# A spectral mixer with an MLP on one core: the first batch's transform as one product, and work moved to GpSimd

## The chip, the cores and the metric

The kernel runs on one core of one Trainium2 chip. The metric is device time in microseconds: the median of three runs is 2610.31 us (2610.21 to 2612.57). The engines are TensorE (PE; PEld is its weight load), VectorE (DVE), ScalarE (ACT), GpSimd (POOL) and SyncE (SP), which here only issues DMAs.

## The reference

For each of 8 batches `x` (3072 positions by 256 channels) goes through a Fourier transform along the positions, a complex 256x256 channel mix with a bias and a soft threshold, and the inverse transform. Then every position goes through an MLP, 256 to 2048 with softplus, back to 256.

```python
X = np.fft.rfft(x, axis=1)
Yr = Xr @ w_r - Xi @ w_i + b_r
Yi = Xr @ w_i + Xi @ w_r + b_i
Yr = np.sign(Yr) * np.maximum(np.abs(Yr) - 0.01, 0.0)   # Yi likewise
y = np.fft.irfft(Y, n=x.shape[1], axis=1)
h = y @ w_in
g = np.maximum(h, 0.0) + np.log1p(np.exp(-np.abs(h)))
out = g @ w_out
```

## The kernel before

**Stages.** The transform of 3072 = 96 x 32 positions is done in two stages. `s1` transforms along 96; its result is kept in SBUF as `a0` for batch 0 and goes through DRAM (`a_dr`) for the others. `s3` (after `load_a` has gathered one pair of groups, `gp` = 0 to 11, out of `a0` or `a_dr`) transforms along 32 with the constants `g1`; `mix` multiplies with the channel weights, adds the bias (for batch 0 `bias0`) and shrinks; `s4` and `s5` are the way back. `s5` leaves tokens, each split into a rounded high and a low fp32r part.

**MLP.** It runs in keys (batch, block pair, one eighth of the hidden width), four steps a key: `slot_products` issues the first product and softplus, `slot_second` the second product. Each product is three matmuls, high x high, high x low, low x high (`mm3`, L249 to L252). First products are Strassen-like: seven combinations of weights and tokens. After batch 0's start the MLP's products fill PE, and the transform of later batches is strewn between.

**Weights.** `w_in` and `w_out` arrive as 64-bit words and are turned into fp32 high and low parts by `split_w`, a generator that goes on one `yield` per step: L196 to L203 take the words apart into two summands `t` and `u`, L219 to L223 add them (with the Strassen combinations of w_in in L228 to L231), L233 rounds the high part, L235 takes the low part, and the result is stored to DRAM, from where later keys stream it. The table `turns` gives for each weight the step at which its conversion begins and at which it is loaded. While `early` holds (steps before -1), the adds of L219 to L223 run on POOL and the product of L203 on DVE; from then on the adds run on DVE and L203 on POOL.

**First transform.** Batch 0 and the columns from 10 on of batch 1, and all later batches, use `s1_four`: x is loaded as two halves of 48 rows, partitions 0 to 47 and 64 to 111 (`load_first`, `load_four`; a memset clears partitions 32 to 63), `fold` makes their sum and difference on DVE (L324, L325, 112x512), and eight matmuls with 48 rows follow (L339). For batch 0, `load_first` finds each of eight loads a place in a buffer that is free at the start. The first eight to ten columns of batch 1 use `s1`, one 96-row product with the constants `f_sb` (L281). ACT copies the results (L348 into `a0`, L283, L352).

**What sets the order.** Everything is written out step by step: `product` puts a transform's matmuls at a step, `at` puts loads, folds and other calls at a step, and the loop at the end of the kernel issues, in each step, the MLP's products, the conversions, the transform product, then what `at` put there. Each engine and each DMA queue works in that order. Steps before 0 are the first batch's transform; `t0` is the first step. SP's queue carries nearly all DMAs; POOL's queue carries half of the `a0` loads from gp 3 on and half of `s4`'s results.

Lines that matter below: L197 (first DVE instruction of a conversion), L478 and L475 (first `z` of a mix: bias added, gp 0 and later), L119 (low part of a split), L378 (`s3`), L362 (`load_a`), L596 and L612 (low parts of tokens), L694 (`add`, one input in PSUM), L710 (`low`, both inputs in SBUF).

Of the kernel before, what the change touches and what calls it, by code (L numbers as in the profile page):

```python
# [10 lines left out]
F32 = mybir.dt.float32  # L11
# [6 lines left out]
P = 128  # L18
# [16 lines left out]
def tile_spectral_mixer_mlp(ctx, tc, x, w_r, w_i, bias, bias_0, w_in, w_out, f, f_hi, f_lo, g1, g3, g3_hi, g3_lo, hm, out):  # L35
# [34 lines left out]
    y1 = sb.tile([P, 14 * BLK], F32, tag="y1", name="y1", bufs=1)  # L70
    a1 = y1[:N1, :4 * 512].rearrange("p (i n) -> p i n", i=4)
    g1_0 = y1[:, 4 * 512:10 * 512].rearrange("p (g n) -> p g n", g=NG)
# [109 lines left out]
    def split_w(which, m2, own):  # L182
# [29 lines left out]
        ahead = bool(early)  # L212
        e = g if ahead else v
        if which:

            tm, um = [a.rearrange("p (k m n) -> p m k n", k=2, m=2) for a in (t, u)]
            a21 = tm[:, 1, 0]
            o = [src[:, i * P:(i + 1) * P] for i in range(7)]
            e.tensor_tensor(out=src[:, A11 * P:(A11 + 2) * P].rearrange("p (k n) -> p k n", k=2), in0=tm[:, 0], in1=um[:, 0], op=ALU.add)  # L219
            e.tensor_tensor(out=a21, in0=a21, in1=um[:, 1, 0], op=ALU.add)  # L220
            e.tensor_tensor(out=o[A22], in0=tm[:, 1, 1], in1=um[:, 1, 1], op=ALU.add)
        else:
            e.tensor_tensor(out=src, in0=t, in1=u, op=ALU.add)  # L223
        if ahead:
            yield
            yield
# [40 lines left out]
    def load_x(b, c):  # L267

        xt = sb.tile([P, 512], F32R, tag=("gh", "gl")[c % 2], name="xt", bufs=3).bitcast(F32)[:N1]
        nc.sync.dma_start(  # L270
            xt.rearrange("p (n c) -> p n c", n=2),
            x[b].rearrange("(p n) c -> p n c", n=N2)[:, 2 * c:2 * c + 2, :],
        )
        xs[b, c] = xt

    def s1(b, c):

        if c == 0:
            a_dr[b] = dram.tile([N1, N2, D], F32, tag="a", name="a_dr")
        ps = psf()  # L280
        nc.tensor.matmul(ps, f_sb, xs.pop((b, c)), start=True, stop=True)  # L281
        a = a1[:, c % 4] if c < 8 else g1_0[:N1, 4 * (c - 8) + 16:4 * (c - 8) + 20].rearrange("p g n -> p (g n)")
        nc.scalar.copy(a, ps[:N1, :])  # L283
        store(a_dr[b][:, 2 * c:2 * c + 2, :], a.rearrange("p (n c) -> p n c", n=2), ("a", b))

# [10 lines left out]

    def load_first(c):

        place = ('w64', 'raw', 'w64', 'l', 'x1', 'w1', 'w1', 'dpt')[c]
        if place == "x1":  # L300
            xt = fours[1]
        elif place == "dpt":
            xt = dpt
        elif place == "raw":
            xt = sb.tile([P, 1024], F32, tag="raw", name="x4", bufs=1)
        elif place == "w64":
            xt = sb.tile([P, 1024], F32, tag="w64", name="x4")
        elif place == "l":
            xt = sb.tile([P, 2 * 768], F32R, tag="l", name="x4", bufs=1).bitcast(F32)
        else:  # L310
            xt = sb.tile([P, 2 * 7 * P], F32R, tag="w1", name="x4").bitcast(F32)
        s = sb.tile([P, 512], F32, tag=("a", "d")[c % 2], name="plus")
        rows = x[0].rearrange("(h p n) c -> p h n c", h=2, n=N2)
        nc.vector.memset(xt[32:64, :1024], 0.0)
        for i in (1, 0):
            n = 4 * c + 2 * i
            nc.sync.dma_start(xt[64 * i:64 * i + 48, :1024].rearrange("p (h n c) -> p h n c", h=2, n=2), rows[:, :, n:n + 2, :])
        xs[0, c, "four"] = xt[:, :512], xt[:, 512:1024], s

    def fold(b, c):  # L320

        lo, hi, both = [t[:112] for t in xs[b, c, "four"]]
        e = nc.vector
        e.tensor_tensor(out=both, in0=lo, in1=hi, op=ALU.add)  # L324
        e.tensor_tensor(out=hi, in0=lo, in1=hi, op=ALU.subtract)  # L325
        stored["x", b, c] += 1

    def s1_four(b, c):
# [4 lines left out]
        _, minus, plus = xs.pop((b, c, "four"))  # L333
        if b:
            stored["four", c % 2] += 1
        banks = psf(), psf()
# [8 lines left out]
        for i, ps in enumerate(banks):  # L345
            n = 4 * c + 2 * i
            if b == 0:
                nc.scalar.copy(a0[:, n:n + 2, :].rearrange("p n c -> p (n c)"), ps)  # L348
                stored["a", b] += 1
                continue  # L350
# [433 lines left out]
    with tc.manual_schedule():  # L784
        nc.scalar.preload_act_table_set("softplus")


        fill, steps, before = {}, {}, {}
        nc.sync.dma_start(f2, f_hi)
        nc.gpsimd.dma_start(g3_sb, g3)  # L790
# [39 lines left out]

        first = [("s1", 0, c) for c in range(8)] + [("s1", 1, c) for c in range(4)]
        for i in range(NP + 3):
# [10 lines left out]
        for t, (what, b, i) in enumerate(first, t0):  # L843
            if what == "s1" and b == 0:
                product(t, s1_four, b, i)
                at(t0 - 1, load_first, i)
            elif what == "s1":
# [24 lines left out]
        last = first.index(("s4", 0, NP - 1)) + t0
        begun = first.index(("s4", 0, 7)) + t0
# [56 lines left out]
def _constants():  # L930
# [95 lines left out]
```

## Time and profile before

| | |
|---|---|
| median of 3 runs | 2610.31 us (2610.21 to 2612.57) |
| profiled execution | span 2607.2 us (the page gives no other time of it) |
| PE busy | 2566.7 us, 98% |
| DVE busy | 1687.6 us, 65% |
| ACT busy | 1669.9 us, 64% |
| POOL busy | 167.0 us, 6% |
| mean granted clock of TensorE | 0.998 |

The profile is of one execution. Times are us from the span's start. "Idle before <-X" is the time that an engine stood before an instruction, and what ended it. A busy PE is not PE at its peak. PEclk is the share of full speed that was granted to TensorE.

### The profile page before, as it was taken

How to read it: one execution, taken by the hardware profiler on the slowest of the kernel's cores; microseconds unless marked ns; L12 is line 12 of the kernel's file. 1: busy time of each engine (PE TensorE's matmuls, PEld its weight loads, DVE VectorE, ACT ScalarE, POOL GpSimd, SP SyncE). 2: the span in 40 equal slices, each digit the busy share in tenths (PEclk: the TensorE clock that was granted, in tenths of full speed). 3: DMA queues.
4: the chain of work that ended last, by engine and by line, in shares of the span. 5: the costliest groups of instructions: out<-in, count | busy, mean ns of one | idle time of the engine just before them, and what ended most of it. 6: DMA issues, size and time to landing. Idle time of an engine off the chain costs nothing.

```text
span 2607.2 us, 36350 instructions
## 1 busy us (share of the span) xinstructions
PE 2566.7 (98%) x13193; PEld 2125.6 (82%) x13193; DVE 1687.6 (65%) x2836; ACT 1669.9 (64%) x3025; POOL 167.0 (6%) x198
## 2 busy tenths in 40 slices
PE   7899999999999999999999999999999999999999
PEld 5677878888788888888888888888888888888887
DVE  6888775676566765667656667466774666645454
ACT  4576666666666666666666666666666666666665
POOL 2320000000000000000000000000000000000000
PEclk9999999999999999999999999999999999999999
DMA  8975555755546556475555665556645545445543
GB/s 214 273 238 193 173 187 164 220 174 176 186 162 199 181 173 190 162 205 179 170 191 174 186 195 163 180 176 187 207 155 173 182 155 190 140 159 183 174 150 113
DMA packets 187087, 472.56 MB, mean 181 GB/s; under 512 B 22252, under 2 KB 88844, under 8 KB 186908
## 3 DMA queue, kind: packets, MB, share of 16 engines
q1 hardware_dynamic: 183084, 466.79, 56.9%
q0 software_dynamic: 2912, 2.58, 0.4%
q8 instruction: 105, 1.72, 0.3%
q10 hardware_dynamic: 912, 0.85, 0.1%
q14 instruction: 74, 0.61, 0.1%
HBM read 383.09 MB, written 82.71 MB: 179 GB/s over the span
## 4 chain that ended last, share of the span: by engine, by line
PE 93%; DVE 3%; DMA 2%; ACT 1%; issue 1%; SPq 0%; ACTq 0%; POOL 0%; DVEq 0%
PE pso L250 14%; PE pso L252 13%; PE pso L251 13%; PE psc L250 7%; PE psc L252 7%; PE psc L251 7%; PE pse L250 5%; PE pse L252 5%; PE pse L251 5%; PE psf L573 5%; PE psf L252 3%; PE psf L251 3%; PE psf L250 3%; PE psf L378 3%; PE psf L339 2%
## 5 line engine op out<-in xcount | busy, mean ns | idle before, releaser
L710 DVE TENSOR_TENSOR gl<-t,gh 128x512 fp32r<-128x512 f32 x768 | 532.2, 693 | 328.9 <-ACT gh L704 326.5
L689 ACT COPY t<-psc 128x512 f32<-128x512 f32 x576 | 337.2, 585 | 524.3 <-PE psc L252 521.8
L694 DVE TENSOR_TENSOR t<-pse,t 128x512 f32<-128x512 f32 x576 | 396.1, 688 | 402.3 <-ACT t L689 276.4
L250 PE MATMUL pso<-gh,w 128*128 128x512 f32 x1536 | 620.6, 404 | 0.0
L252 PE MATMUL pso<-gh,w 128*128 128x512 f32 x1536 | 599.5, 390 | 0.0
L251 PE MATMUL pso<-gl,w 128*128 128x512 f32 x1536 | 599.2, 390 | 0.0
L704 ACT CAST gh<-t 128x512 fp32r<-128x512 f32 x768 | 476.8, 621 | 60.8 <-PE pso L252 37.4
L700 ACT ACTIVATE t<-t 128x512 f32<-128x512 f32 x576 | 365.1, 634 | 69.2 <-DVE t L694 68.0
L250 PEld LDWEIGHTS pso<-gh,w 128*128 128x128 f32 x1536 | 289.3, 188 | 90.6 <-issue 41.4
L252 PEld LDWEIGHTS pso<-gh,w 128*128 128x128 f32 x1536 | 288.3, 188 | 62.5
L251 PEld LDWEIGHTS pso<-gl,w 128*128 128x128 f32 x1536 | 289.4, 188 | 49.2
L250 PE MATMUL psc<-y_sb,w 128*128 128x512 f32 x768 | 300.9, 392 | 5.4 <-ACT t L689 5.1
L252 PE MATMUL psc<-y_sb,w 128*128 128x512 f32 x768 | 299.9, 391 | 0.0
L251 PE MATMUL psc<-y_sb,w 128*128 128x512 f32 x768 | 299.1, 389 | 0.0
L612 POOL TENSOR_TENSOR y_sb<-raw,y_sb 128x512 fp32r<-128x512 f32 x69 | 104.9, 1520 | 2147.4 <-ACT y_sb L609 2147.4
L250 PE MATMUL pse<-y_sb,w 128*128 128x512 f32 x576 | 226.2, 393 | 4.4 <-DVE t L694 4.4
L251 PE MATMUL pse<-y_sb,w 128*128 128x512 f32 x576 | 224.5, 390 | 0.6 <-DVE y_sb L596 0.6
L252 PE MATMUL pse<-y_sb,w 128*128 128x512 f32 x576 | 224.4, 390 | 0.0
L250 PEld LDWEIGHTS psc<-y_sb,w 128*128 128x128 f32 x768 | 144.2, 188 | 38.7 <-ACT t L689 7.9
L252 PEld LDWEIGHTS psc<-y_sb,w 128*128 128x128 f32 x768 | 144.3, 188 | 31.2
L251 PEld LDWEIGHTS psc<-y_sb,w 128*128 128x128 f32 x768 | 144.4, 188 | 30.0
L511 DVE TENSOR_TENSOR shrunk<-z,cl 64x256 f32<-64x256 f32 x336 | 141.1, 420 | 6.2
(168 smaller groups left out, 3365.1 us busy)
## 6 DMA issues: line engine op xcount, KB each, us to landing
w<-w_dr SPq DMA_DIRECT2D x190, 896.0 KB, 7.6
w<-w_dr SPq DMA_DIRECT2D x185, 512.0 KB, 3.5
out_y<-ot SPq DMA_DIRECT2D x96, 256.0 KB, 2.8
x<-in_x SPq DMA_DIRECT2D x116, 192.0 KB, 7.3
dp<-d_dr SPq DMA_DIRECT2D x57, 384.0 KB
ap<-a_dr SPq DMA_DIRECT2D x168, 128.0 KB, 6.0
d_dr<-d SPq DMA_DIRECT2D x84, 256.0 KB, 2.1
a_dr<-a SPq DMA_DIRECT2D x102, 192.0 KB, 3.0
```

The source lines that it names most:

```text
L250: nc.tensor.matmul(ps, wh, xh, start=start, stop=False, skip_group_check=more)
L251: nc.tensor.matmul(ps, wh, xl, start=False, stop=False, skip_group_check=more)
L252: nc.tensor.matmul(ps, wl, xh, start=False, stop=stop, skip_group_check=more)
L378: nc.tensor.matmul(xv[:, g, k], t[:, g, k * P:(k + 1) * P], g1_t[:, g].rearrange("p (c s) -> p c s", c=2), start=True, stop=True,)
L511: v.tensor_tensor(out=t[dst], in0=z[src], in1=cl[src], op=ALU.subtract)
L573: nc.tensor.matmul(ps[:, t - blk * BLK:t - blk * BLK + n], d_sb[b, blk // 2, n2 // 4][0][:, n2 % 4, k * P:(k + 1) * P], d_sb[b, blk // 2, ...
L612: eng.tensor_tensor(out=lo, in0=raw[j], in1=hi.bitcast(F32), op=ALU.subtract)
L689: nc.scalar.copy(t, banks[bank])
L694: nc.vector.tensor_tensor(out=t, in0=banks[bank], in1=t, op=ALU.add)
L700: nc.scalar.activation(t, banks[bank] if bank else t, AF.Softplus)
L704: nc.scalar.copy(gh, ct[key, what])
L710: nc.vector.tensor_tensor(out=gl, in0=ct.pop((key, what)), in1=gh.bitcast(F32), op=ALU.subtract)
```

## The change

- Batch 0's first transform uses `s1`, 16 products of 96 rows with `f_sb`, in place of eight times `s1_four`. `load_first`, its memsets and its folds are gone. The 16 loads of x go to 96 partitions each, at places of their own: `xt` buffers, the `dp` buffer, and `x1`; four of them are issued by ACT. `f` is padded by 16 columns, so that the results lie in partitions 16 to 111 as before.
- `t0` is 8 steps earlier (16 products in place of 8). The loads of `g1`, `bias0`, the mix's weights and `f2` stand at other steps; ACT's table load stands behind its DMA issues.
- `fold` runs on POOL for batches 1 and 2.
- The adds of `split_w` run on POOL also for conversions inside the MLP, and what follows the adds comes one step later there.

```diff
-    a1 = y1[:N1, :4 * 512].rearrange("p (i n) -> p i n", i=4)
+    a1 = y1[:16 + N1, :4 * 512].rearrange("p (i n) -> p i n", i=4)
...
         ahead = bool(early)
-        e = g if ahead else v
+        e = g
...
             e.tensor_tensor(out=src, in0=t, in1=u, op=ALU.add)
+        yield
         if ahead:
-            yield
             yield
         if which:
             v.tensor_tensor(out=o[S1], in0=a21, in1=o[A22], op=ALU.add)
...
     def load_x(b, c):
-        xt = sb.tile([P, 512], F32R, tag=("gh", "gl")[c % 2], name="xt", bufs=3).bitcast(F32)[:N1]
-        nc.sync.dma_start(
+        if b or c < 6:
+            xt = sb.tile([P, 512], F32R, tag=("gh", "gl")[c % 2], name="xt", bufs=3).bitcast(F32)
+        elif c < 14:
+            xt = dps[:, (c - 6) * 512:(c - 5) * 512]
+        else:
+            xt = fours[1][:, (c - 14) * 512:(c - 13) * 512]
+        xt = xt[:N1]
+        (nc.sync if b or c % 2 == 0 or c > 8 else nc.scalar).dma_start(
             xt.rearrange("p (n c) -> p n c", n=2),
...
         nc.tensor.matmul(ps, f_sb, xs.pop((b, c)), start=True, stop=True)
+        if b == 0:
+            nc.scalar.copy(a0[:, 2 * c:2 * c + 2, :].rearrange("p n c -> p (n c)"), ps)
+            stored["a", b] += 1
+            return
...
-    def load_first(c):
...
     def fold(b, c):
         lo, hi, both = [t[:112] for t in xs[b, c, "four"]]
-        e = nc.vector
+        e = nc.gpsimd if b < 3 else nc.vector
...
-        nc.scalar.preload_act_table_set("softplus")
-        nc.sync.dma_start(f2, f_hi)
+        nc.sync.dma_start(f_sb, f)
...
-        first = [("s1", 0, c) for c in range(8)] + [("s1", 1, c) for c in range(4)]
+        first = [("s1", 0, c) for c in range(16)] + [("s1", 1, c) for c in range(4)]
...
-                at(max(t0 - 1, t - (5 if i < 4 else 16)), load_x, b, i)
+                at(t - 16 if b and i >= 4 else t0 + 4 + i if b else t0 - 1, load_x, b, i)
...
-                at(max(t - 7, t0 + 8), load_a, b, i)
+                at(max(t - 7, t0 + 16), load_a, b, i)
...
-        for c in range(8):
-            at(max(t0 - 1, t0 + c - 1), fold, 0, c)
-        for t, i, j in ((t0 + 7, 0, 4), (t0 + 8, 4, 12), (t0 + 14, 12, NG)):
+        for t, i, j in ((t0 + 7, 0, 4), (t0 + 18, 4, 12), (t0 + 20, 12, NG)):
             at(t, nc.sync.dma_start, g1_0[:, i:j], g1[:, NG + i:NG + j])
-        at(t0 + 5, nc.sync.dma_start, bias0, bias_0)
+        at(t0 + 19, nc.sync.dma_start, bias0, bias_0)
         at(12, nc.sync.dma_start, bias_sb, bias)
         for k in range(2):
-            at(t0 + 6 + k, load_mix, k)
-            at(t0 + 10 + k, split_mix, k)
-        at(t0 + 2, nc.sync.dma_start, f_sb, f)
+            at(t0 + 10 + k, load_mix, k)
+            at(t0 + 17 + k, split_mix, k)
+        at(-30, nc.sync.dma_start, f2, f_hi)
...
+        at(t0 - 1, nc.scalar.preload_act_table_set, "softplus")
...
-    f = np.pad(f, ((0, 0), (0, P - N1)))
+    f = np.pad(f, ((0, 0), (16, P - N1 - 16)))
```

SP's queue between batch 0's x and the first conversion, before. `x_96` holds `f_sb` and `bias0`, `y_79` holds `g1_0` and the results of batch 1's `s1`, `ap` receives the `a0` loads (source `a_78`), `dpt` a weight.

```order
L914 DMA x_96<-in_f 96x128
L270 DMA xt<-in_x 96x512 x3
L914 DMA x_96<-in_bias 128x512
L270 DMA xt<-in_x 96x512
L145 DMA stage<-in_w_r 128x2x256
L914 DMA y_79<-in_g 128x512
L145 DMA stage<-in_w_i 128x2x256
L362 DMA ap<-a_78 128x1x256 x6
L914 DMA y_79<-in_g 128x1024
L179 DMA dpt<-in_w_in 128x2x512
```

The same queue in the changed kernel.

```order
L889 DMA y_79<-in_g 128x512
L145 DMA stage<-in_w_r 128x2x256
L145 DMA stage<-in_w_i 128x2x256
L344 DMA ap<-a_78 128x1x256 x6
L179 DMA dpt<-in_w_in 128x2x512
L104 DMA a_dr<-y_79 96x512
L344 DMA ap<-a_78 128x1x256
L889 DMA y_79<-in_g 128x1024
L104 DMA a_dr<-y_79 96x512
L889 DMA x_96<-in_bias 128x512
L104 DMA a_dr<-y_79 96x512
L889 DMA y_79<-in_g 128x1536
```

The bias load moved from ahead of the six `a0` loads to behind them, and the second part of `g1` from ahead of the first `w_in` load to behind it.

DVE at the start of batch 0's mixes, before: the last fold, the splits of the mix's weights, the low part of the first s3, the first `z`, `cl` and difference, the next low part, and the first conversion.

```order
L325 TENSOR_TENSOR dpt<-dpt 112x512
L119 TENSOR_TENSOR wml<-stage,wmh 128x2x256 x2
L119 TENSOR_TENSOR w_277<-psf,w_277 128x4x128
L478 TENSOR_TENSOR z<-psf,x_96 128x512
L479 TENSOR_SCALAR cl<-z 128x512
L480 TENSOR_TENSOR z<-z,cl 128x512
L119 TENSOR_TENSOR w_287<-psf,w_287 128x4x128
L197 TENSOR_SCALAR wt<-dpt 128x512
```

DVE in the changed kernel, from its first instruction.

```order
L119 TENSOR_TENSOR wml<-stage,wmh 128x2x256 x2
L119 TENSOR_TENSOR w_229<-psf,w_229 128x4x128
L460 TENSOR_TENSOR z<-psf,x_96 128x512
L461 TENSOR_SCALAR cl<-z 128x512
L462 TENSOR_TENSOR z<-z,cl 128x512
L119 TENSOR_TENSOR w_239<-psf,w_239 128x4x128
L197 TENSOR_SCALAR wt<-dpt 128x512
```

The memsets and folds in front are gone; from the splits on, the sequence is the same.

POOL from the last conversion that begins before the MLP, before. `x_96` and `x_97` are the two buffers of `s1_four`'s x.

```order
L219 TENSOR_TENSOR y_79<-wt,wu 128x256
L220 TENSOR_TENSOR wt<-wt,wu 128x128
L221 TENSOR_TENSOR y_79<-wt,wu 128x128
L914 MEMSET x_96 32x1024
L203 TENSOR_TENSOR wu<-y_79,wu 128x512 x4
L158 TENSOR_TENSOR stage<-stage 128x512
```

POOL at the same place in the changed kernel.

```order
L311 TENSOR_TENSOR x_97<-x_97 112x512
L312 TENSOR_TENSOR x_97<-x_97 112x512
L889 MEMSET x_96 32x1024
L203 TENSOR_TENSOR wu<-y_79,wu 128x512
L219 TENSOR_TENSOR y_79<-wt,wu 128x256
L220 TENSOR_TENSOR wt<-wt,wu 128x128
L221 TENSOR_TENSOR y_79<-wt,wu 128x128
L311 TENSOR_TENSOR x_96<-x_96 112x512
L312 TENSOR_TENSOR x_96<-x_96 112x512
L311 TENSOR_TENSOR x_97<-x_97 112x512
L312 TENSOR_TENSOR x_97<-x_97 112x512
L203 TENSOR_TENSOR wu<-y_79,wu 128x512
```

Between the products of L203 stand the folds (L311, L312) and the adds that DVE had.

## Rows read from the trace of the kernel before

**Rows 1.** Windows by stage: each engine's busy us (instructions), PEclk, DMA share, GB/s.
```profile
0.00:109.00 109.00, 86.83 (x542) 65.91 (x542) 82.36 (x139) 51.55 (x102) 33.80 (x60) 0.98 0.84 229
109.00:125.00 16.00, 9.99 (x33) 5.83 (x31) 15.38 (x26) 11.49 (x21) 3.77 (x4) 0.89 1.01 346
125.00:260.00 135.00, 128.90 (x651) 100.80 (x652) 114.30 (x202) 95.80 (x175) 20.06 (x21) 1.00 0.68 218
260.00:2607.20 2347.20, 2340.97 (x11971) 1953.06 (x11970) 1475.60 (x2471) 1511.09 (x2730) 109.38 (x114) 1.00 0.56 176
```

**Rows 2.** The chain that ended last, start: begin, us, what (DMAs to landing).
```profile
12.03 8.25 DMA dpt<-in_x
...
31.32 8.77 DMA dpt<-in_w_in
```

**Rows 3.** Windows of the start: PE, PEld, DVE, ACT, POOL busy, PEclk, DMA share, GB/s.
```profile
4.00:20.00 16.00, 9.78 (x54) 4.21 (x56) 13.89 (x20) 5.79 (x12) 0.00 (x0) 1.00 1.08 195
20.00:26.00 6.00, 5.51 (x22) 1.85 (x16) 1.38 (x2) 3.95 (x8) 0.00 (x0) 1.00 0.93 281
26.00:30.00 4.00, 1.93 (x10) 1.04 (x8) 1.39 (x2) 2.42 (x6) 0.01 (x1) 1.00 0.27 96
```

**Rows 4.** Timeline of the first 32 us: begin, us, instruction, count, [idle before <-releaser].
```profile
10.22 1.12 PE L339 MATMUL psf<-plus,f 48*64 48x512 f32 x2 [10.22 <-DVE plus L324]
...
15.39 1.06 PE L339 MATMUL psf<-plus,f 48*64 48x512 f32 x2
...
17.21 0.59 PE L339 MATMUL psf<-plus,f 48*64 48x512 f32 x2
...
22.84 3.70 PE L281 MATMUL psf<-xt,x 96*128 96x512 f32 x8
...
24.04 5.78 SPq L362 DMA_DIRECT2D ap<-a  x6
```

**Rows 5.** Timeline from 34 to 46 us, the first two mixes.
```profile
36.99 0.69 DVE L478 TENSOR_TENSOR z<-psf,x 128x512 f32<-128x512 f32 x1 [6.00 <-PE psf L252]
...
38.69 1.13 PE L378 MATMUL psf<-y,ap 128*128 128x128 f32 x8 [1.74 <-issue]
...
38.87 0.68 DVE L119 TENSOR_TENSOR w<-psf,w 128x512 fp32r<-128x512 f32 x1
...
40.11 0.43 DVE L197 TENSOR_SCALAR wt<-dpt 128x512 uint32<-128x512 uint32 x1 [0.55 <-DMA dpt<-in_w_in]
...
43.24 0.68 DVE L475 TENSOR_TENSOR z<-psf,x 128x512 f32<-128x512 f32 x1
...
45.98 0.39 PE L252 MATMUL psf<-wmh,w 128*128 128x256 f32 x1 [1.10 <-DVE w L119]
```

**Rows 6.** Timeline of DVE at 86 us.
```profile
86.22 0.43 DVE L197 TENSOR_SCALAR wt<-w 128x512 uint32<-128x512 uint32 x1 [2.18 <-DMA w<-in_w_out]
```

**Rows 7.** DMA issues from 1.0 to 1.7 us: KB each, us to landing.
```profile
x<-in_x SPq DMA_DIRECT2D x1, 192.0 KB, 3.4
```

**Rows 8.** Windows from 30 to 42 us, columns as in rows 3.
```profile
30.00:34.00 4.00, 3.60 (x14) 3.13 (x14) 0.69 (x1) 1.44 (x4) 1.82 (x3) 0.57 0.60 187
34.00:42.00 8.00, 5.99 (x46) 5.61 (x47) 4.16 (x7) 2.25 (x5) 1.29 (x6) 1.00 0.96 277
```

**Rows 9.** Timeline of DVE at 108 us.
```profile
108.44 0.89 DVE L324 TENSOR_TENSOR x<-x 112x512 f32<-112x512 f32 x1
```

**Rows 10.** DVE's fold (L324), then adds (L223; DVE, POOL), in the fill.
```profile
125.00:260.00 135.00, 4.09 (x6) 1.00 0.68 218
...
125.00:260.00 135.00, 4.50 (x5) 0.00 (x0) 1.00 0.68 218
```

**Rows 11.** One line's instructions, ns min/median/max, first and last start: L203 POOL, L710.
```profile
L203 POOL TENSOR_TENSOR wu<-y,wu x5: 1305/1313/1548, 122.7 to 170.4; 128x512 f32<-128x512 f32 x5
...
L710 DVE TENSOR_TENSOR gl<-t,gh x768: 672/692/1800, 118.4 to 2598.5; 128x512 fp32r<-128x512 f32 x192
```

**Rows 12.** Timeline of DVE at 122 us.
```profile
122.72 1.80 DVE L710 TENSOR_TENSOR gl<-t,gh 128x512 fp32r<-128x512 f32 x1 [0.29 <-ACT gh L704]
```

More of the change, by code (lines that the diff above doesn't have):

```diff
@@ L281, in s1 @@
         nc.tensor.matmul(ps, f_sb, xs.pop((b, c)), start=True, stop=True)
-        a = a1[:, c % 4] if c < 8 else g1_0[:N1, 4 * (c - 8) + 16:4 * (c - 8) + 20].rearrange("p g n -> p (g n)")
-        nc.scalar.copy(a, ps[:N1, :])
-        store(a_dr[b][:, 2 * c:2 * c + 2, :], a.rearrange("p (n c) -> p n c", n=2), ("a", b))
+        if b == 0:
+            nc.scalar.copy(a0[:, 2 * c:2 * c + 2, :].rearrange("p n c -> p (n c)"), ps)
+            stored["a", b] += 1
+            return
+        a = a1[:, c % 4] if c < 8 else g1_0[:16 + N1, 4 * (c - 8) + 16:4 * (c - 8) + 20].rearrange("p g n -> p (g n)")
+        nc.scalar.copy(a, ps[:16 + N1, :])
+        store(a_dr[b][:, 2 * c:2 * c + 2, :], a[16:].rearrange("p (n c) -> p n c", n=2), ("a", b))
     def load_four(b, c):
@@ L295, in load_four @@
         xs[b, c, "four"] = [xt[:, 512 * i:512 * i + 512] for i in range(3)]
-    def load_first(c):
[L299 to L318, printed above, removed]
     def fold(b, c):
         lo, hi, both = [t[:112] for t in xs[b, c, "four"]]
-        e = nc.vector
+        e = nc.gpsimd if b < 3 else nc.vector
         e.tensor_tensor(out=both, in0=lo, in1=hi, op=ALU.add)
@@ L333, in s1_four @@
         _, minus, plus = xs.pop((b, c, "four"))
-        if b:
-            stored["four", c % 2] += 1
+        stored["four", c % 2] += 1
         banks = psf(), psf()
@@ L346, in s1_four @@
             n = 4 * c + 2 * i
[L347 to L350, printed above, removed]
             a = sb.tile([P, 512], F32, tag="a", name="a")
@@ L843, in tile_spectral_mixer_mlp @@
         for t, (what, b, i) in enumerate(first, t0):
[L844 to L847, printed above, removed]
+            if what == "s1":
                 product(t, s1, b, i)
-                at(max(t0 - 1, t - (5 if i < 4 else 16)), load_x, b, i)
+                at(t - 16 if b and i >= 4 else t0 + 4 + i if b else t0 - 1, load_x, b, i)
             elif what == "s3":
                 product(t, s3, b, i)
-                at(max(t - 7, t0 + 8), load_a, b, i)
+                at(max(t - 7, t0 + 16), load_a, b, i)
             elif what == "mix":
```

## The prediction

> **What bounds the kernel now.** I read the busy time by stretch first, then the start in order of time. The profiled span is 2607.2 us [rows 1]; the three timed runs have a median of 2610.31 us, so 3.1 us lie around it, and I add every change to 2610.31. TensorE (PE) is busy 2340.97 of 2347.20 us from 260 us on; it idles 6.1 us between 125 and 260, 6.0 us between 109 and 125, and 22.2 us in the first 109 [rows 1]. So the change can win only before 260 us: in the first batch's transform (to 109) and in the fill of the MLP (109 to 260), where VectorE (DVE) is busy 15.38 of 16 and 114.30 of 135 us.
>
> The start has four pieces. The x loads: the last lands at 12.03 + 8.25 = 20.28 us [rows 2]; from 4 to 20 us the DMA engines are full (share 1.08) and move 195 GB/s, and from 20 to 26 us, with loads into 96 or 128 partitions in place of 48, 281 GB/s at a share of 0.93 [rows 3]. The transform: PE begins at 10.22, released by a DVE fold; its pieces take 1.06 us at 15.39 and 0.59 us at 17.21, so it runs at the lower of its two clock levels (1.2 GHz) for some 6 us of work and at 2.4 GHz after; the first a0 load is issued at T = 24.04 [rows 4]. Six a0 loads then move 96 GB/s at a share of 0.27 [rows 3]; behind them SP issues 512 KB of g1 and, at 31.32, 512 KB of w_in, landed at 40.09 [rows 2]. Last, the chain that sets the pace [rows 5]: PE's third s3 at 38.69 after 1.74 us of idling, for which only the g1 transfer is left (its other operand was issued before it); DVE's first z at 36.99, its L119 at 38.87, the weight conversion from 40.11, the second z at 43.24, and a PE product that waits 1.10 us for DVE at 45.98. What is late at the second z is late for the whole batch. Later DVE stands 2.18 us for a w_out load, until 86.22 [rows 6].
>
> **The change, term by term.**
>
> *a0 ready.* Eight memsets and sixteen DVE folds go, and PE no longer waits for them. The first x load took 3.4 us from its issue at about 1.2 [rows 7], so PE can start at 4.6. At 281 GB/s a 192 KB load takes 0.70 us, so the sixteenth lands at 15.1. The new product is that of L281, where eight records (four products) take 3.70 us [rows 4], 0.86 us each; at the lower level twice that, 1.72. With 6.2 us at the lower level: 3.6 products until 10.8, the other 12.4 in 10.7 us, to 21.5, and a copy of 0.5 to T = 22.0: -2.0 us. Bounds: full clock at once, 4.6 + 13.8 + 0.5 = 18.9 (-5.1); the level rises no earlier than before, at about 16.3, then 6.8 products are done by it, the rest ends at 24.2, T = 24.7 (+0.7). PE is the limit here; the loads hide behind it.
>
> *g1 and bias_0 behind the w_in load.* SP is one queue. Before, bias_0 and all other constants but g1[4:] stood ahead of the a0 loads. Now behind the six a0 loads come w_in, a 192 KB store, a 128 KB a0 load, g1[4:12], another store, and only then bias_0. Before, a0 loads + g1 + w_in were through at 40.09 = T + 16.05. To the new end of g1 there are 320 KB more, to that of bias_0 768 KB more; at 277 GB/s (34 to 42 us [rows 8]) this is 1.2 and 2.8 us. With T = 22.0: g1 at 39.3, bias_0 at 40.9. The first z needs bias_0 (36.99 before), and queued behind z on DVE are L119, for which PE's second mix waits, and the conversion, for which the second z waits. From the first z to the end of L119 is 39.55 - 36.99 = 2.6 us, from the conversion to the second z 43.24 - 40.11 = 3.1 [rows 5]: second z at 40.9 + 5.7 = 46.6 against 43.24, **+3.4 us**, of which T gives -2.0 and the wait +5.4. Bounds: nothing late, -5.1 with T at its end; the 768 KB at only 195 GB/s [rows 3], bias_0 at T + 20.1 from T = 24.7, second z at 50.5, +7.3. I take the middle, since it is one queue's sum at the rate of that very stretch. Were bias_0 in time, g1 alone would put the second z at 39.3 + (43.24 - 38.69) = 43.9 at most, which is still no gain.
>
> *Carried to 109.* PE and DVE are both nearly full from the second z to the end of the batch, so a delay is passed on, save where a DMA is waited for: up to the 2.18 us before 86.22 [rows 6]. I take 1.0 off (0 to 2.2): +2.4.
>
> *Start of the MLP.* The first fold of batch 1 leaves DVE at 108.44 (two instructions of about 0.9 us, the first in [rows 9]), but the instruction behind it there waits for ScalarE (ACT) as well, and the fold now runs on GpSimd (POOL) just when DVE reads what POOL's adds made. I take -0.5 (-1.8 to +0.6).
>
> *The fill.* Between 125 and 260 DVE loses six folds (two times 4.09 us), five w_out adds (4.50) [rows 10] and three sets of w_in adds (as many elements, 0.69 us a set): about 15 us. POOL gets them: a 128x512 instruction takes 1.31 us there against 0.69 on DVE [rows 11]; 12 fold instructions and eight sets make some 26 us. DVE does not keep its 15 us: at 122.72 an L710 with both inputs in SBUF took 1.80 us beside a POOL instruction [rows 12], against a median of 0.69 [rows 11], 1.1 us lost. Half of that for each of 26 instructions (a w_in set has three) is 14 us, a wash. I take 0 for PE (-2.0 to +2.5). The extra yield puts the conversions one step later: products of w_out weights 3 to 6 come two steps after their low part and hide it; weight 7's low part now falls in the step of its product, at most two DVE instructions of 0.69 us, once: +0.3 (0 to 1.4). Folds after 260 cost nothing: PE is full there, and DVE is busy 1475.60 of 2347.20 us [rows 1].
>
> The Trainium skill ("SBUF — State Buffer", section "Who interferes with whom") says that a VectorE instruction with two SBUF inputs and a GpSimd one that reads SBUF exclude each other for a whole instruction, while one with a PSUM input goes on. The row at 122.72 agrees. By that rule, with every moved instruction stopping DVE for all of its own time, DVE would be 26 - 15 = 11 us busier where it has 20.7 us free; the sum would then go to the slower rival.
>
> Sum: +2.4 - 0.5 + 0 + 0.3 = **+2.2 us, 2612.5**, no change that can be told: 0.2% is 5.2 us, about what a measurement of this kernel can tell from none.
>
> **The rivals.**
>
> *Slower: a longer gap lowers the clock, and POOL holds DVE.* From 26 to 30 us PE is busy 1.93 of 4 us [rows 3], and from 30 to 34 its granted clock is 0.57 [rows 8]. The change opens a longer gap: the first mix is done some 2 us earlier, g1 comes at 39.3, L119 ends only at 43.5. At 1.2 GHz the s3 and mix behind it, 4.55 us at most (38.69 to 43.24 [rows 5]), take as much again; about half of it shows, +2.4. With the fill at its +2.5: 2612.5 + 4.9 = 2617.4. It decides once bias_0 lands after about 40. Against it: from 34 to 42 the clock was full [rows 8] although PE stood 1.74 us there.
>
> *Faster: nothing is late.* If the transfers behind w_in overtake it and the clock rises early: -3.5 at the second z, -1.2 at the MLP's start, -1.8 in the fill, 2603.8. For it: DVE is the fullest engine of these stretches. Against: six a0 loads at 96 GB/s stand in front of everything.
>
> *Only the first gain arrives:* bias_0 and g1 land in time, the rest as forecast: -2.0 - 0.5 + 0.3, 2608.1, within 0.2% too.
>
> **How the numbers follow.** Forecast 0.52, only the first gain 0.10, slower rival 0.27, faster rival 0.11. So faster 0.11, within 0.2% 0.62, slower 0.27. The forecast's own range is 2608 to 2615.5; leaving out some 0.1 on each side gives 2605.5 to 2619.5, into both rivals.
>
> **What would show it.** In the changed kernel's trace: x loads at about 280 GB/s from 4 to 15 us; PE's transform from about 4.6 and the first a0 load at about 22; the first z (now L460) ending a wait on the bias_0 transfer at about 41, the third s3 at about 39, the second z (L457) at about 46.6; POOL busy about 85 us before 260 in place of 58; L692 (the old L710) at 1.2 us and more beside POOL's sums; PE's idle time between 125 and 260 still near 6. It is wrong if the first z does not wait for bias_0, if T is not before 24, or if PE's idle time in the fill falls by more than 2 us.

## The result and the profile after

The changed kernel is slower: median 2630.38 us (2627.18 to 2633.12, four runs) against 2610.26 us (2609.0 to 2612.57) of the kernel before, ratio 1.0072, 95% interval 1.0059 to 1.0085. The profiled execution has a span of 2629.1 us, 21.9 us more than before.

Windows of the changed kernel, the same stretches and columns as [rows 1]:

```profile
0.00:109.00 109.00, 86.62 (x454) 66.58 (x455) 58.31 (x103) 46.55 (x91) 28.71 (x53) 0.92 0.73 210
109.00:125.00 16.00, 11.58 (x66) 8.21 (x64) 11.81 (x23) 10.58 (x19) 8.68 (x12) 0.99 0.88 289
125.00:260.00 135.00, 120.65 (x579) 92.10 (x581) 112.20 (x166) 90.09 (x163) 51.09 (x46) 0.96 0.64 212
260.00:2629.10 2369.10, 2360.76 (x12069) 1968.35 (x12067) 1486.69 (x2487) 1525.26 (x2754) 123.11 (x124) 1.00 0.56 176
```

PE idles 14.35 us between 125 and 260 (6.1 before) and 8.3 us after 260 (6.2 before). DVE's busy time in the fill has hardly fallen, 112.20 us after 114.30, although 15 us of work left it. POOL's rose from 20.06 to 51.09.

Windows at fixed times hide that the work has shifted. To place the loss I set the same event of both traces side by side. One event can be counted through the whole MLP: ScalarE's cast `gh`, the high part of a softplus result (L704 before, L686 after), 768 times in each. The 1st and the 35th in ScalarE's timeline, first of the kernel before, then of the changed one (begin, us, instruction):

```profile
116.42 0.62 ACT L704 CAST gh<-t 128x512 fp32r<-128x512 f32 x1
...
236.32 0.62 ACT L704 CAST gh<-t 128x512 fp32r<-128x512 f32 x1
```
```profile
125.76 0.62 ACT L686 CAST gh<-t 128x512 fp32r<-128x512 f32 x1
...
256.63 0.62 ACT L686 CAST gh<-t 128x512 fp32r<-128x512 f32 x1
```

| same event | before, us | after, us | late by | forecast |
|---|---|---|---|---|
| second `z` | 43.24 | 48.50 | 5.3 | 3.4 |
| 1st `gh` | 116.42 | 125.76 | 9.3 | 1.9 |
| 35th `gh` (fill over) | 236.32 | 256.63 | 20.3 | 2.2 |
| 47th `gh` | 281.92 | 300.93 | 19.0 | 2.2 |
| 76th `gh` | 390.08 | 411.31 | 21.2 | 2.2 |
| end of the span | 2607.2 | 2629.1 | 21.9 | 2.2 |

So there are three losses: 9.3 us ahead of the MLP, 11.0 in the fill, 2.1 around 380 us; 1.3 come back at a wait that PE had before at 258 us, and 0.8 are lost in smaller steps.

The windows from the 1st to the 35th `gh` hold the same work, first before, then after:

```profile
116.42:236.32 119.90, 112.98 (x558) 86.63 (x557) 104.83 (x184) 86.40 (x155) 21.37 (x22) 0.99 0.71 231
125.76:256.63 130.87, 116.52 (x558) 88.88 (x557) 108.10 (x160) 86.67 (x155) 51.09 (x46) 0.97 0.63 208
```

Of the 11.0 us that the fill loses, 7.4 are more idle time of PE (14.35 us, 6.92 before), and 3.5 are the same 558 matmul records taking longer (granted clock 0.97 after 0.99). DVE's busy time went up from 104.83 to 108.10 us.

**The start.** DVE's timeline from 40 to 49 us:

```profile
40.77 0.69 DVE L460 TENSOR_TENSOR z<-psf,x 128x512 f32<-128x512 f32 x1 [12.47 <-DMA x<-in_bias]
...
42.66 0.68 DVE L119 TENSOR_TENSOR w<-psf,w 128x512 fp32r<-128x512 f32 x1
...
48.50 0.69 DVE L457 TENSOR_TENSOR z<-psf,x 128x512 f32<-128x512 f32 x1 [2.03 <-PE psf L252]
```

The first `z` stood 12.47 us and was released by the transfer of bias_0. Before, it began at 36.99, released by PE [rows 5]. PE idled 5.42 us ahead of the third s3, and its granted clock then fell; PE's line, then the windows:

```profile
39.67 2.05 PE L360 MATMUL psf<-y,ap 128*128 128x128 f32 x8 [5.42 <-issue]
```
```profile
34.00:42.00 8.00, 2.58 (x13) 2.25 (x11) 1.10 (x2) 0.00 (x0) 0.00 (x0) 0.83 0.94 341
42.00:46.00 4.00, 2.74 (x13) 2.60 (x13) 3.68 (x8) 2.31 (x5) 0.68 (x1) 0.50 0.44 140
```

The second mix runs at 1.2 GHz (granted clock 0.50), so that the second `z` waits 2.03 us for PE (no wait in [rows 5]). Later the DMA wait before a w_out conversion, 2.18 us in [rows 6], has grown to 4.38:

```profile
93.58 0.43 DVE L197 TENSOR_SCALAR wt<-w 128x512 uint32<-128x512 uint32 x1 [4.38 <-DMA w<-in_w_out]
```

Last, PE waits longer ahead of the MLP's first products, 4.27 us where it was 3.32. PE before and after, then DVE and POOL after:

```profile
114.91 0.50 PE L250 MATMUL psc<-y_sb,w 128*128 128x512 f32 x1 [3.32 <-ACT t L689]
```
```profile
124.24 0.51 PE L250 MATMUL psc<-y_sb,w 128*128 128x512 f32 x1 [4.27 <-ACT t L671]
```
```profile
119.82 1.24 DVE L231 TENSOR_TENSOR y<-y 128x128 f32<-128x128 f32 x1
```
```profile
119.49 1.42 POOL L311 TENSOR_TENSOR x<-x 112x512 f32<-112x512 f32 x1 [1.04 <-DMA x<-in_x]
```

One short sum on DVE, 0.28 us alone, took 1.24 us beside the first fold on POOL.

**The fill.** PE's two longest waits here, from its timeline:

```profile
225.53 0.50 PE L250 MATMUL pse<-y_sb,w 128*128 128x512 f32 x1 [2.44 <-DVE t L676]
...
240.58 0.69 PE L252 MATMUL pso<-gh,w 128*128 128x512 f32 x1 [2.81 <-DVE w L235]
```

What DVE and POOL did ahead of the first (two timelines, same stretch):

```profile
221.85 1.36 DVE L119 TENSOR_TENSOR l<-sum,l 128x256 fp32r<-128x256 f32 x1
223.13 1.75 DVE L692 TENSOR_TENSOR gl<-t,gh 128x512 fp32r<-128x512 f32 x1
224.80 0.68 DVE L676 TENSOR_TENSOR t<-pse,t 128x512 f32<-128x512 f32 x1
```
```profile
221.62 1.30 POOL L223 TENSOR_TENSOR w<-wt,wu 128x512 f32<-128x512 f32 x1
222.88 1.45 POOL L311 TENSOR_TENSOR x<-x 112x512 f32<-112x512 f32 x1
224.41 1.60 POOL L312 TENSOR_TENSOR x<-x 112x512 f32<-112x512 f32 x1
```

L119 and L692, with both inputs in SBUF, run only when the POOL instruction beside them is over (1.36 and 1.75 us with that wait; alone 0.4 and 0.69). L676 reads PSUM and takes its usual 0.68 beside L312. PE waits for L676, which stood behind the held ones in DVE's order. Ahead of the second wait it is four `shrunk` in front of the low part (L235). DVE and POOL after, then the same four on DVE before:

```profile
234.93 3.67 DVE L493 TENSOR_TENSOR shrunk<-z,cl 64x256 f32<-64x256 f32 x4
```
```profile
234.57 1.47 POOL L311 TENSOR_TENSOR x<-x 112x512 f32<-112x512 f32 x1
236.12 1.34 POOL L312 TENSOR_TENSOR x<-x 112x512 f32<-112x512 f32 x1
```
```profile
220.19 1.72 DVE L511 TENSOR_TENSOR shrunk<-z,cl 64x256 f32<-64x256 f32 x4
```

They took 3.67 us beside two folds and 1.72 without. (0.9 us of that wait come with the extra step alone, in before_step.) Behind both waits the clock falls: the granted clock is 0.59 from 228 to 231 us and again from 240 to 244, and the matmul at 240.58 takes 0.69 us, not 0.39.

**At 380 us** one fold on POOL stands beside two short DVE instructions that PE needs at once. DVE, then POOL, then PE:

```profile
379.19 1.51 DVE L119 TENSOR_TENSOR l<-sum,l 128x256 fp32r<-128x256 f32 x1 [0.71 <-ACT l L375]
380.63 1.75 DVE L119 TENSOR_TENSOR sl<-shrunk,sh 128x512 fp32r<-128x512 f32 x1
```
```profile
379.13 1.30 POOL L311 TENSOR_TENSOR x<-x 112x512 f32<-112x512 f32 x1 [23.97 <-DMA x<-in_x]
380.51 1.33 POOL L312 TENSOR_TENSOR x<-x 112x512 f32<-112x512 f32 x1
```
```profile
382.44 0.50 PE L251 MATMUL psf<-sl,g3h 128*128 128x512 f32 x1 [1.85 <-DVE sl L119]
```

The same two took 0.43 and 0.69 us in the kernel before.

### The profile page after: what moved, and what is told of

It is laid out like the page before. It is cut to its first block, busy times and chain, and to the rows that moved or that the text cites. A ratio compares the mean times of both kernels' runs of the same rounds, so it can differ in the third digit from the quotient of the medians.

```text
span 2629.1 us, 36272 instructions
## 1 busy us (share of the span) xinstructions
PE 2579.6 (98%) x13161; PEld 2135.2 (81%) x13161; DVE 1669.0 (63%) x2776; ACT 1672.5 (64%) x3025; POOL 211.6 (8%) x234
## 4 chain that ended last, share of the span: by engine, by line
PE 93%; DVE 3%; DMA 2%; ACT 1%; SPq 1%; issue 1%; ACTq 0%; DVEq 0%
PE pso L250 14%; PE pso L252 13%; PE pso L251 13%; PE psc L250 6%; PE psc L252 6%; PE psc L251 6%; PE pse L250 5%; PE pse L251 5%; PE pse L252 5%; PE psf L555 4%; PE psf L252 3%; PE psf L251 3%; PE psf L250 3%; PE psf L360 3%; PE psf L325 2%; PE psf L287 1%
## 5 line engine op out<-in xcount | busy, mean ns | idle before, releaser
L692 DVE TENSOR_TENSOR gl<-t,gh 128x512 fp32r<-128x512 f32 x768 | 536.8, 699 | 332.8 <-ACT gh L686 330.3
L676 DVE TENSOR_TENSOR t<-pse,t 128x512 f32<-128x512 f32 x576 | 396.5, 688 | 406.1 <-ACT t L671 277.3
L686 ACT CAST gh<-t 128x512 fp32r<-128x512 f32 x768 | 477.1, 621 | 60.8 <-PE pso L252 37.4
```

What stands on the lines that cost most here:

```text
L676: nc.vector.tensor_tensor(out=t, in0=banks[bank], in1=t, op=ALU.add)
L686: nc.scalar.copy(gh, ct[key, what])
L692: nc.vector.tensor_tensor(out=gl, in0=ct.pop((key, what)), in1=gh.bitcast(F32), op=ALU.subtract)
```

## The experiments

Medians in us; ratios to the kernel before, timed beside each group of runs (medians 2610.17 to 2611.07).

| run | median | ratio (95%) |
|---|---|---|
| only_transform | 2619.65 | 1.0030 (1.0019 to 1.0041) |
| early_bias | 2626.47 | 1.0055 (1.0042 to 1.0067) |
| fold_dve | 2623.56 | 1.0043 (1.0029 to 1.0056) |
| adds_dve | 2632.03 | 1.0071 (1.0058 to 1.0083) |
| bias_late_alone | 2618.34 | 1.0029 (1.0017 to 1.0040) |
| transform_early_bias | 2610.92 | 1.0003 (0.9994 to 1.0011) |
| transform_g1_first | 2610.42 | 1.0001 (0.9992 to 1.0010) |
| pool_alone | 2621.97 | 1.0045 (1.0031 to 1.0058) |
| before_fold | 2621.53 | 1.0043 (1.0031 to 1.0056) |
| before_adds | 2616.97 | 1.0024 (1.0014 to 1.0034) |
| before_step | 2613.54 | 1.0010 (1.0002 to 1.0019) |
| before_fold_pieces | 2613.14 | 1.0007 (0.9998 to 1.0015) |
| g1_first_fold_pieces | 2612.22 | 1.0010 (1.0001 to 1.0019) |
| first_fold_pool | 2610.04 | 1.0000 (0.9991 to 1.0009) |
| first_fold_pieces | 2609.81 | 0.9998 (0.9989 to 1.0007) |
| g1_first_x_early | 2610.87 | 1.0003 (0.9994 to 1.0012) |
| before_pool_pieces | 2610.73 | 1.0003 (0.9994 to 1.0012) |
| g1_first_pool_pieces | 2610.62 | 1.0003 (0.9994 to 1.0012) |

### Undoing one part

**early_bias.**

```diff
-        for t, i, j in ((t0 + 7, 0, 4), (t0 + 18, 4, 12), (t0 + 20, 12, NG)):
+        for t, i, j in ((t0 + 7, 0, 4), (t0 + 16, 4, 12), (t0 + 20, 12, NG)):
-        at(t0 + 19, nc.sync.dma_start, bias0, bias_0)
+        at(t0 + 13, nc.sync.dma_start, bias0, bias_0)
```

> The changed kernel with two loads moved: bias_0 to a step ahead of the a0 loads, g1[4:12] to right behind them. Theory: the late bias_0 causes all of the 9.3 us that the changed kernel is behind at the MLP's first gh, the later DMA wait and the slower clock included. Then the first z ends no wait on bias_0, the second z comes at about 41 to 43 us in place of 48.5, the first gh near 117 in place of 125.8, and the time is 2630.4 - 9 = 2621 (2619 to 2624). Rival: the wait before the w_out conversion (4.4 us) is DMA throughput and stays; then the second z is early, the first gh still 3 to 4 us late, and the time 2625. Rival: PE's wait for the second part of g1, not bias_0, sets the second z: then it stays near 47 and the time at 2628 or more.

3.9 us came back of 9 (20.1 us over the kernel before became 15.4). The first `z` no longer waits for bias_0, but in the profiled execution the transform's products became fast late, and the first a0 load was issued at 25.33 us (21.36 in the changed kernel), the second `z` at 45.3. The first `gh` is still 5.6 us late, and PE's wait ahead of the MLP's first products is 4.86 us there.

**fold_dve** (first edit), **adds_dve** (second) and **only_transform** (both):

```diff
-        e = nc.gpsimd if b < 3 else nc.vector
+        e = nc.vector
```
```diff
-        e = g
+        e = g if ahead else v
...
-        yield
         if ahead:
+            yield
             yield
```

> The changed kernel with all folds on DVE again, nothing else. Theory: a fold on POOL holds DVE instructions that PE is about to need; without it the 2.1 us at 380 us are gone (L119 there takes 0.43 and 0.69 us, not 1.51 and 1.75), and of PE's waits in the fill those at 222.7 (2.4 us) and 237.8 (2.8 us) with the slower clock behind each (some 1.8 us): 2630.4 - 2.1 - 5 to 8 = 2620 to 2623. Rival (the forecast's wash): DVE pays for the folds itself in the fill what it is now held; only the 2.1 us at 380 come back: 2628. Rival: the adds and not the folds are the cost: 2628 to 2630.

> The changed kernel with the adds of conversions inside the MLP on DVE again and without the extra step, as in the kernel before; folds stay on POOL. Theory (folds hold DVE): only the waits on the low parts go (1.7 us at 217.4, part of 2.8 us at 237.8) with the clock that falls behind: 2630.4 - 3 to 5 = 2625 to 2627, and the 2.1 us at 380 stay. Rival (the adds are the cost): 2630.4 - 8 to 11 = 2619 to 2622. Rival (the wash): 2629 to 2631.

> The changed kernel with both undone: folds on DVE, adds on DVE without the extra step. What is left of the change is the whole-array transform with its loads and queue. Theory (losses of the start stay, those of the fill and at 380 go): 2610.3 + 9.3 = 2619.6 (2617 to 2622). Rival: a late start is made up in the fill where DMA and DVE have slack: 2612 to 2615. Rival: the late start also costs in the fill: 2624 or more.

Folds back on DVE: 6.8 us regained. Adds back alone: nothing in the median (five runs from 2626.2 to 2632.57), where 3 to 5 us were expected. Both back: 2619.65, the 2619.6 expected (seven runs from 2617.55 to 2621.08). In that trace every `gh` from the 6th to the 417th is 9.5 to 9.8 us later than before, and 10.7 to 11.6 from there to the end: no loss in the fill, none at 380 us, and no late start made up.

### One part alone

**transform_early_bias** is only_transform with the edit of early_bias; **transform_g1_first** also loads g1[4:12] at `t0 + 13`, ahead of the a0 loads. **bias_late_alone** puts into the kernel before

```diff
-        for t, i, j in ((t0 + 7, 0, 4), (t0 + 8, 4, 12), (t0 + 14, 12, NG)):
+        for t, i, j in ((t0 + 7, 0, 4), (t0 + 10, 4, 12), (t0 + 12, 12, NG)):
-        at(t0 + 5, nc.sync.dma_start, bias0, bias_0)
+        at(t0 + 11, nc.sync.dma_start, bias0, bias_0)
```

> The kernel before with only bias_0 and g1[4:12] loaded where the changed kernel loads them, behind the a0 loads and w_in. Theory (the queue alone makes the start late): the first z waits for bias_0 until about 43 (T is 24, 19.4 us later as in the changed kernel), the second z at about 51, the time 2610.7 + 6 to 9 = 2617 to 2620. Rival (the lateness is made up before the MLP): 2611 to 2613.

> The whole-array transform alone (folds and adds on DVE), with bias_0 ahead of the a0 loads and g1[4:12] right behind them. Theory (the parts add up): moving the two loads was worth 3.9 us beside POOL's work and is worth the same here: 2619.65 - 3.9 = 2615.7 (2614 to 2618); the second z at 43 to 45.5 us, the first gh still 4 to 6 us later than before. Rival (bias_0 is all of the start's loss, and the 4 us were only part of it because POOL hid the rest): 2611 or less.

> As transform_early_bias, but g1[4:12] also stands ahead of the a0 loads, so that it moves while PE still transforms and w_in comes right behind the a0 loads. Theory: with both out of the way PE does not wait at the third s3, its clock does not fall there, and the first z is set by the first mix, at about T + 12.5: second z at about 41 (43.24 before), the time 2 to 4 us under transform_early_bias, 2611 to 2614. Rival (some 3.5 us between the second z and the first gh belong to the whole-array transform whatever the loads do, and T is late in many executions since the clock rises late): no gain over transform_early_bias, 2615 to 2617. A gain over the kernel before needs under 2608.

The late loads alone cost 7.6 us with the old transform. DVE's first `z` in that trace:

```profile
43.21 0.69 DVE L478 TENSOR_TENSOR z<-psf,x 128x512 f32<-128x512 f32 x1 [11.57 <-DMA x<-in_bias]
```

With the two loads in time the whole-array transform costs nothing: 2610.92, the rival's number, where I had expected 2615.7. It gains nothing either. In transform_g1_first the second `z` comes at 40.7 us, 2.6 earlier than before, but the first `gh` only 0.2 earlier; DVE waits for transfers in between, 0.7 us more for a w_out load than in [rows 6] and 1.85 for an x:

```profile
84.41 0.43 DVE L197 TENSOR_SCALAR wt<-w 128x512 uint32<-128x512 uint32 x1 [2.89 <-DMA w<-in_w_out]
...
108.57 0.69 DVE L311 TENSOR_TENSOR x<-x 112x512 f32<-112x512 f32 x1 [1.85 <-DMA x<-in_x]
```

**pool_alone** is the kernel before with folds and adds of the changed one, **before_fold**, **before_adds** and **before_step** its parts (folds; adds with the extra step; the step alone, with the adds on DVE).

> The kernel before with the fold of batches 1 and 2 and all adds on POOL with the extra step; its transform and its loads are untouched. Theory (the fill's loss does not depend on the start): 2610.7 + 10.8 = 2621.5 (2619 to 2624), with PE waits of 1.7, 2.4 and 2.8 us for DVE in the fill and one of 1.9 us for DVE's sl after it. Rival (a wash, the waits come from the late start): 2610 to 2613.

> The kernel before with only the folds of batches 1 and 2 on POOL. Theory (POOL's folds hold DVE instructions that PE waits for): a wait of 1.5 us more at the MLP's start, some 6.5 us in the fill less 1.3 regained behind it, and 1 to 2 us at the fold near 370 us: 2611 + 7 to 9 = 2618 to 2620. Rival (the adds are the larger part, the folds only matter beside them): 2612 to 2615.

> The kernel before with only the adds of all conversions on POOL and the extra step behind them. Theory: 6.8 us in the fill, as the changed kernel with its folds on DVE showed between 125 and 245 us: 2611 + 5 to 7 = 2616 to 2618. Rival (the parts cost only together): 2611 to 2613.

> The kernel before with only the extra step ahead of what follows the adds; the adds stay on DVE. Theory (a low part that comes in the step of its product makes PE wait): a wait of about 1.7 us for the low part of a w_in weight near 211 us stays, with the slower clock behind it; 2611 + 2 to 3.5 = 2613 to 2614.5, and the rest of what before_adds loses is POOL holding DVE. Rival (the step is hidden, as forecast: 0.3 us): 2611. Rival (the step is nearly all of it): 2616 or more.

pool_alone loses 11.2 us. From the 1st to the 35th `gh` it loses 11.0, the changed kernel's 11.0, with the same waits of 1.7, 2.4 and 2.8 us: the fill's loss does not come from the late start. The parts do not add up. Folds alone cost 10.9, adds with the step 6.4, the step 2.9; together 11.2. They overlap: PE waits for one and the same L694 2.52 us with the folds alone, 2.44 with the adds alone and 2.44 with both (at 217.5 to 219.5 us). Beside the folds the adds cost 0.3 us (11.2 after 10.9), which fits adds_dve. The step's wait, on PE in before_step:

```profile
208.34 0.50 PE L252 MATMUL psc<-y_sb,w 128*128 128x512 f32 x1 [1.71 <-DVE w L235]
```

### Is it the whole POOL instruction that DVE waits for?

**before_fold_pieces** is before_fold with each fold in four pieces; **g1_first_fold_pieces** has the same on transform_g1_first. The arithmetic and POOL's elements are the same.

```diff
-        e.tensor_tensor(out=both, in0=lo, in1=hi, op=ALU.add)
-        e.tensor_tensor(out=hi, in0=lo, in1=hi, op=ALU.subtract)
+        n = 4 if 0 < b < 3 else 1
+        for w in [slice(512 // n * j, 512 // n * (j + 1)) for j in range(n)]:
+            e.tensor_tensor(out=both[:, w], in0=lo[:, w], in1=hi[:, w], op=ALU.add)
+            e.tensor_tensor(out=hi[:, w], in0=lo[:, w], in1=hi[:, w], op=ALU.subtract)
```

> As before_fold, but each fold in four pieces of 128 columns (eight POOL instructions in place of two). Theory (a DVE instruction with both inputs in SBUF waits for the end of one POOL instruction, and gets its turn between two): what is held is at most a piece, about a quarter of 1.3 us, and the loss falls from 10.9 us to 2 to 5: 2613 to 2616. Rival (POOL takes the rate away, or its next piece always comes first): 2619 to 2623, as before_fold.

> transform_g1_first with the folds of batches 1 and 2 on POOL in four pieces each. Theory: as before_fold_pieces, 2 to 5 us over transform_g1_first: 2612 to 2615. Rival (with short pieces DVE's relief shows): 2606 to 2608. Rival (pieces change nothing): 2620.

10.9 us become 2.9, which is no longer clear of the kernel before, and the rival (pieces change nothing) falls; with the other transform 2612.22 comes out, at the low end of what was expected. The windows from 125 to 260 us, before_fold and then before_fold_pieces (an execution of 2609.19 us, under its median):

```profile
125.00:260.00 135.00, 125.28 (x617) 97.28 (x616) 108.48 (x177) 91.82 (x166) 38.91 (x34) 0.97 0.66 211
```
```profile
125.00:260.00 135.00, 128.23 (x650) 100.43 (x643) 109.38 (x184) 94.93 (x172) 47.26 (x69) 1.00 0.66 214
```

POOL is busy 8 us longer with the pieces, PE idles 6.8 us in place of 9.7 and keeps its clock. How DVE gets its turn, before_fold_pieces, POOL and DVE:

```profile
208.69 0.56 POOL L327 TENSOR_TENSOR x<-x 112x128 f32<-112x128 f32 x1
209.21 0.90 POOL L326 TENSOR_TENSOR x<-x 112x128 f32<-112x128 f32 x1
```
```profile
208.84 0.95 DVE L712 TENSOR_TENSOR gl<-t,gh 128x512 fp32r<-128x512 f32 x1
209.72 0.68 DVE L696 TENSOR_TENSOR t<-pse,t 128x512 f32<-128x512 f32 x1
```

The low part takes 0.95 us where whole folds made it 1.75, and now POOL's next piece is the one that waits (0.90 for about 0.45). No such run was made for the adds: that the 3.5 us by which they exceed the step are holds too is read from the traces and not shown by a run.

### Looking for a faster version

**first_fold_pool** has transform_g1_first's one fold that stands for its x (108.57 above) on POOL, **first_fold_pieces** that fold in pieces, **g1_first_x_early** loads that x three steps earlier instead (and clears its buffer four steps earlier). **before_pool_pieces** cuts POOL's own 128x512 instructions inside the MLP in four, in the kernel before, and **g1_first_pool_pieces** does so in first_fold_pieces.

```diff
-        e = nc.gpsimd if b < 3 else nc.vector
+        e = nc.gpsimd if (b, c) == (1, 5) else nc.vector
```
```diff
-                at(-8 if (b, c) == (1, 5) else t - 7, load_four, b, c)
+                at(-11 if (b, c) == (1, 5) else t - 7, load_four, b, c)
```

> transform_g1_first with one fold on POOL, the first of batch 1, which there stands on DVE for 1.85 us waiting for its x, ahead of the low part that PE then waits 2.3 us for. Theory (a fold on POOL pays where it waits and nothing on DVE is held): the wait at the MLP's start shrinks by 1.5 to 2.3 us and the time to 2608 to 2609, 0.7 to 1 per mille under the kernel before. Rival (that low part is then held by the fold itself, or PE waits for the same x a little later): 2610.4, no change.

> As first_fold_pool (only the first fold of batch 1 on POOL, the rest of transform_g1_first), with that fold in four pieces. Theory: PE's wait at the MLP's start falls from 4.9 us to 3.3, as with the fold on DVE, without DVE's wait for x: 2608 to 2609. Rival: 2610, as first_fold_pool.

> transform_g1_first with batch 1's first x for s1_four loaded three steps earlier (its memset four steps), all folds on DVE. Theory (DVE stood 1.85 us for that x, and the low part behind it made PE wait 2.3 us): that wait goes and the time is 2608 to 2609. Rival (PE then waits for the adds or for batch 0's last stage at the same place): 2610.4.

> The kernel before, with nothing moved: POOL's 128x512 sums and products inside the MLP (L203, L612, and L158 and L119 on POOL) in four pieces of 128 columns. Theory (a DVE instruction waits for the whole POOL instruction beside it): of the 6 us that PE idles between 125 and 260 us, the waits behind a held DVE instruction go, 1 to 3 us: 2607.5 to 2609.5. Rival (those waits are DVE's own order and ScalarE's): 2610.4. Rival (shorter pieces make POOL itself late): slower than 2611.

> first_fold_pieces with the same cut of POOL's instructions. Theory: 2609.8 - 1 to 3 = 2607 to 2609, clear of the kernel before. Rival: 2609 to 2611.

All five are within 0.03% of the kernel before: the gains expected of each were missed, and no version is shown to be faster. Cutting POOL's own instructions changes nothing in the kernel before; in that trace PE still idles 5.66 us between 125 and 260 (6.1 before), which fits the rival that those waits are not holds by POOL. In first_fold_pool the wait for x is gone, but the fold holds DVE's short sums ahead of PE's first products, and PE waits 4.94 us there, not 3.32:

```profile
109.33 0.83 DVE L228 TENSOR_TENSOR y<-wt,y 128x128 f32<-128x128 f32 x1
...
110.28 1.35 DVE L230 TENSOR_TENSOR y<-y 128x128 f32<-128x128 f32 x1
```
```profile
115.14 0.80 PE L250 MATMUL psc<-y_sb,w 128*128 128x512 f32 x1 [4.94 <-ACT t L671]
```

## Why the prediction was wrong

**The step that failed is "The fill ... a wash. I take 0 for PE (-2.0 to +2.5)".** Its working for DVE came near: 15 us of relief against 14 held, and over the same work DVE was busy 108.10 us in place of 104.83. But PE does not wait for DVE's sum. It waits for single instructions, and some of those that were held stand just ahead of what PE needs. The relief is there as well (a wait of PE of 0.95 us at 156.62 became 0.16), but it is smaller. The forecast even had DVE free for 20.7 us in this stretch, and there a relief is worth little and a hold of 1.1 us at the wrong place is worth its length, and more once the clock falls. The fill lost 11.0 us in the trace in place of 0; pool_alone, which has all of POOL's work and the old start, costs 11.2 us in all. The Trainium skill ("SBUF — State Buffer", section "Who interferes with whom") states that such instructions exclude each other for a whole one and that the one issued first wins. The pieces agree for the folds: 10.9 us became 2.9. I had cited the rule and used it for a sum of busy time. None of the three signs of being wrong that were named came up; the idle time of PE in the fill, said to stay near 6 us, went to 14.35.

**"Folds after 260 cost nothing"** was wrong for the same reason: PE is full there, but its cover at one place was less than 2.2 us of held DVE (2.1 us at 380).

**"Start of the MLP ... -0.5"** had the wrong sign for that reason too: the fold that left DVE held a short sum of DVE there, and PE's wait grew by 0.95 us (4.86 us in before_fold, 3.33 in before_adds, 3.32 before).

**"Extra yield +0.3 (0 to 1.4)"** looked at the low part of w_out weight 7 only; PE waits for that one too (0.9 us in before_step), but longer, 1.7 us, for the low part of w_in weight 7 (128x896), which I had left out, with five DVE instructions ahead of it in that step and not two. The step alone measured 2.9 us (ratio 1.0010, 1.0002 to 1.0019).

**The start: mechanism right, size too small.** All of the start together was 9.3 us late at the first `gh` where 1.9 was forecast. x moved at 281 GB/s from 4 to 15 us, PE began at 4.90, the first a0 load came at 21.36 (forecast 22.0), the first `z` ended its wait for bias_0 at 40.77 (40.9), the third s3 began at 39.67 (39). That bias_0 came out within 0.2 us is in part luck: the first a0 load was 0.6 us early, and the transfers behind it took 19.4 us where 18.9 was forecast. From first to second `z` I carried over 5.7 us; it took 7.73, since the clock had fallen (0.50 from 42 to 46 us). That was the slower rival's mechanism, with 2.0 us measured for its 2.4. Alone, the late loads cost 7.6 us.

**"Carried to 109: -1.0" had the wrong sign.** Between the second `z` and the first `gh` 4.1 us were added, 2.2 of them at the wait of [rows 6] that was to absorb some. That wait absorbed nothing: the windows from 80 to 100 us have a DMA share near 0.9 in both kernels, which fits a load that lands late when the traffic before it was late, but no run shows it. The wait differs between traces whose loads are untouched (2.32 us in pool_alone, 3.04 in before_fold) and those with bias_0 in time (2.89 in transform_g1_first, 3.74 in transform_early_bias), so only a part of the 2.2 us goes with the lateness; how much was not settled. Some 0.95 us more are the held sum at the MLP's start.

**The slower rival** (2617.4) was the right side, with both its mechanisms at work; it took the fill at 2.5 us, and there the time went past its number and past the range. "Only the first gain arrives" and "nothing is late" were excluded by bias_0.

**What stays open.** The parts overlap: bias_late_alone (7.6) and pool_alone (11.2) add up to 18.8 us, near the change's 20.1. But with the loads in time, POOL's work costs 15.4 us beside the whole-array transform (early_bias) and 11.2 beside the old one, though that transform alone costs nothing. From the 1st to the 95th `gh` the traces differ by 1.0 us only (11.9 lost in early_bias, 10.9 in pool_alone); ahead of the 1st they are 5.6 and 3.3 us late. The transform of the profiled execution of early_bias became fast late; whether its other runs' did, the traces do not show. That the held instructions are the cause is shown for the folds by the pieces; for the adds it is argued.

## What to carry to other kernels

- Work moved to an engine that can hold another's instructions is not priced by busy time. List, for each moved instruction, which DVE instructions stand beside it and who waits for them: one held for 1.1 us just ahead of a product costs PE that, and then the clock.
- When something must run on POOL beside a tight DVE chain, short instructions cost POOL time and spare PE: eight of 128 columns in place of two of 512 took the loss from 10.9 to 2.9 us.
- A constant that a stage needs belongs ahead of slow loads in its queue: two of them (768 KB) behind such loads cost 7.6 us.
- Parts that share a wait do not add up, so try them together and alone.

## What the hardware showed beyond that

- A DVE instruction with one SBUF input was held as well. In before_fold, `cl` (L504) took 1.37 us beside a fold and ends just after it; alone it takes 0.43. The Trainium skill ("SBUF — State Buffer", section "Who interferes with whom") lists this operation among those that can take both ports; the trace agrees. DVE, then POOL:

```profile
229.60 1.37 DVE L504 TENSOR_SCALAR cl<-z 128x512 f32<-128x512 f32 x1
```
```profile
229.40 1.28 POOL L325 TENSOR_TENSOR x<-x 112x512 f32<-112x512 f32 x1
```

- The same 16 products of the transform become fast at different times. ScalarE's copies of them come some 1.7 us apart at first and 0.86 us apart later, and a matmul record takes 1.19 us and then 0.59, the factor between 1.2 and 2.4 GHz, though the granted-clock column shows 1.00 from 4 to 18 us. The last copy at the slow distance begins at 8.69 us in the changed kernel, 10.83 in only_transform and 15.13 in early_bias, which have the same transform. The first a0 load is issued at 21.36, 22.60 and 25.33 us; in early_bias PE also stood 1.01 us for an x load.
